# Last store moved from ScalarE to SyncE and two filler matmuls dropped in a SwiGLU feed-forward kernel

## The chip, the cores and the metric

One core of a Trainium2 chip. The metric is the device time of one execution in microseconds (us); lower is better. A time is the median of several executions, where not said otherwise. A profiled execution gives a span, from the first instruction to the last, which is about 1.3 us shorter than the time of the same execution. A run counts as slow when it is over 1.5% above the fastest of its kernel; the ratios are of fast runs alone, and the state of a single run is unknown.

A few words used below: the sequencer of an engine reads its instructions and starts them. A transfer is issued by an instruction on SyncE or ScalarE, and it has landed when its semaphore (the counter that others wait on) has its last increment. TensorE runs at half or at full clock: the 128-column fillers start 107 ns apart at half clock and 56 ns apart at full clock. The release is the moment at which the full clock is granted.

## The reference

```python
# x: 1 x 2048 x 640; w_gate, w_up: 640 x 1536; w_down: 1536 x 640; all bf16
def reference(x, w_gate, w_up, w_down):
    g = jax.nn.silu(x @ w_gate)
    u = x @ w_up
    return (g * u) @ w_down
```

## The kernel before

The 2048 rows of x are worked in four blocks of 512. In each block TensorE makes the gate tile `pg` and the up tile `pu` for 12 slices of 128 columns, ScalarE applies silu, VectorE multiplies, and TensorE then multiplies by w_down. The first block has no time to wait for a transposing load, so TensorE transposes x itself, and filler matmuls on a tile of ones (`warm`) fill the waits. The parts that matter here are the first and the last ones.

```python
    def warm(n):                      # fillers: their result is never read
        for _ in range(n):
            nc.tensor.matmul(pw[:, 0:P], lhsT=ones[:], rhs=ones[:], start=True, stop=True)
    ...
            if sb == 0 and fc == 0:   # the very first projection
                warm(N_WARM)          # 18
                transpose_chunk(0, [(dve, "po_a", 0, KD)])
                transpose_chunk(2, [(dve, "po_b", 0, KD)])
                warm(N_GAP)           # 2
                for c in (1, 3):
                    transpose_chunk(c, [(act, "po_a", 0, 2), (dve, "po_b", 2, KD)])
                warm(2)               # the two that the change drops
                proj_pair(pg, wg_sb, fc, sb, 0)   # ten matmuls of 256 columns in all
                proj_pair(pg, wg_sb, fc, sb, 1)
                proj(pu, wu_sb, fc, sb, 0, S_BLK)
    ...
        for j in range(SUB):          # output tiles of 128 rows
            ...
            nc.scalar.copy(ot[:], po_a[:])
            nc.sync.dma_start(out=out2[s0 : s0 + P, 0:DA], in_=ot[:])       # wide: 512 columns
            if last:
                # 12 matmuls of 128 columns into po_b
                nc.vector.tensor_copy(out=ot_b[:], in_=po_b[:])
                nc.scalar.dma_start(out=out2[s0 : s0 + P, DA:D], in_=ot_b[:])  # narrow: 128 columns
```

At the end SyncE alone waits for every semaphore (`_trim` moves all closing waits there) and clears them. The load queues are SyncE's and ScalarE's; the first tile of w_gate comes in two parts, three fifths on SyncE, two fifths on ScalarE.

## Time and profile before

| | before |
|---|---|
| time, first three runs | 164.18 us median (163.74 to 164.37) |
| span of the profiled run | 162.8 us |
| TensorE busy | 159.7 us, 98% of the span |
| first projection starts | 5.30 us |
| wide store's issue to the end of the span | 2.05 us |

The costliest groups of the page of before read as follows: line, engine, operation, tiles, shapes and count; then busy us and mean ns of one; then the idle time of the engine just before them and what ended it.

```profile
L198 PE MATMUL pu<-xT,wu_sb 128*128 128x512 bf16 (+1 forms) x240 | 59.5, 379 | 0.0
...
L245 ACT ACTIVATE sg<-pg 128x512 f32<-128x512 f32 (+1 forms) x48 | 28.6, 596 | 70.2 <-PE pg L198 65.7
```

TensorE's matmuls have no idle time before them (0.0). ScalarE sits idle for 70 us, nearly always until TensorE has filled a gate tile. So taking instructions from ScalarE gains nothing in the middle of this kernel; only its part in the very last stretch can count.

### The profile page before, as it was taken

Reading aid. Unit: us, or ns where it says so; the run is one execution under the profiler, and the core shown is the slowest. Engines: PE = TensorE matmul, PEld = TensorE weight load, DVE = VectorE, ACT = ScalarE, POOL = GpSimd, SP = SyncE. Lnnn points to the kernel's source line nnn. Section 1 sums busy time; section 2 is a strip of 40 time slices with the busy share of each in tenths; the row PEclk is TensorE's granted clock in tenths of the full one; section 3 lists DMA queues with packets and bytes.
Section 4 is the critical chain, followed back from the end, with each engine's and each line's share of the span. In section 5 each row is a group of like instructions: output and inputs, shape, how many; then the busy total and the mean of one; then the engine's idle time right before and its main releaser. Section 6 shows DMA issues by size and latency. Waiting matters only on the chain.

```text
span 162.8 us, 2081 instructions
## 1 busy us (share of the span) xinstructions
PE 159.7 (98%) x779; PEld 75.4 (46%) x779; DVE 111.8 (69%) x251; ACT 42.6 (26%) x73; POOL 0.6 (0%) x6
## 2 busy tenths in 40 slices
PE   8999999999999999999999999999999999999994
PEld 7644444444444444444444444444444444445442
DVE  2223333499559999979919999979964999993000
ACT  3322222212232222221222322221214222222121
POOL 1000000000000000000000000000000000000000
DMA  7999999993269993003110000000420000000312
GB/s 212 295 327 330 364 216 253 245 185 60 66 152 180 220 220 68 4 0 34 64 64 0 0 4 2 0 0 0 64 68 32 0 0 0 0 0 4 53 35 73
DMA packets 42585, 15.86 MB, mean 97 GB/s; under 512 B 33232, under 2 KB 42448, under 8 KB 42576
## 3 DMA queue, kind: packets, MB, share of 16 engines
q1 hardware_dynamic: 33664, 14.75, 37.2%
q10 hardware_dynamic: 8912, 0.98, 4.0%
q8 instruction: 6, 0.10, 0.3%
q14 instruction: 3, 0.02, 0.1%
HBM read 7.21 MB, written 2.62 MB: 60 GB/s over the span
## 4 chain that ended last, share of the span: by engine, by line
PE 95%; DMA 3%; SPq 0%; DVE 0%; issue 0%
PE pu L198 32%; PE pg L198 31%; PE po_a L281 25%; PE po_t L256 6%; DMA wg_sb<-in_w_gate_dram 3%; PE pg L213 1%; SPq L84 0%; PE po_b L298 0%; DVE ot_b L306 0%
## 5 line engine op out<-in xcount | busy, mean ns | idle before, releaser
L198 PE MATMUL pu<-xT,wu_sb 128*128 128x512 bf16 (+1 forms) x240 | 59.5, 379 | 0.0
L198 PE MATMUL pg<-xT,wg_sb 128*128 128x512 bf16 (+1 forms) x235 | 58.3, 379 | 0.0
L246 DVE TENSOR_TENSOR aT<-sg,pu 128x512 bf16<-128x512 f32 (+1 forms) x48 | 32.8, 683 | 32.0 <-PE pu L198 32.0
L245 ACT ACTIVATE sg<-pg 128x512 f32<-128x512 f32 (+1 forms) x48 | 28.6, 596 | 70.2 <-PE pg L198 65.7
L281 PE MATMUL po_a<-wd_sb,aT 128*128 128x512 bf16 x192 | 42.1, 379 | 0.0
L151 DVE SCALAR_TENSOR_TENSOR prod<-wgT,x_row 128x640 f32<-128x640 bf16 x48 | 39.4, 821 | 1.1
L151 DVE SCALAR_TENSOR_TENSOR prod<-wuT,x_row 128x640 f32<-128x640 bf16 x48 | 39.4, 821 | 1.0
L198 PEld LDWEIGHTS <-wu_sb 128*128 128x128 bf16 x240 | 23.5, 98 | 28.0
L198 PEld LDWEIGHTS <-wg_sb 128*128 128x128 bf16 x235 | 23.0, 98 | 27.6
L281 PEld LDWEIGHTS <-aT 128*128 128x128 bf16 x192 | 18.8, 98 | 22.5
L289 ACT CAST ot<-po_a 128x512 bf16<-128x512 f32 x16 | 9.4, 586 | 32.3 <-PE po_a L281 21.3
L256 PE MATMUL po_t<-aT,wd_sb 128*128 128x512 bf16 (+1 forms) x48 | 10.4, 366 | 0.0
L256 PEld LDWEIGHTS <-wd_sb 128*128 128x128 bf16 x48 | 4.7, 98 | 5.1
L306 DVE CAST ot_b<-po_b 128x128 bf16<-128x128 f32 x1 | 0.3, 291 | 9.9 <-PE po_b L298 9.9
L265 ACT CAST ot_t<-po_t 128x512 bf16<-128x512 f32 (+1 forms) x4 | 2.2, 560 | 11.6 <-PE po_t L256 11.6
L194 DVE COPY xT<-pt 128x640 bf16<-128x640 bf16 (+1 forms) x4 | 1.6, 425 | 3.4 <-PE pt L189 3.4
L151 DVE DVE_READ_ACCUMULATOR prod<-wuT,x_row 128x1 f32 x48 | 3.9, 82 | 0.0
L151 DVE DVE_READ_ACCUMULATOR prod<-wgT,x_row 128x1 f32 x48 | 3.9, 82 | 0.0
L267 DVE STREAM_TRANSPOSE ot_q<-ot_t 128x512 bf16<-128x512 bf16 (+1 forms) x4 | 2.7, 678 | 1.7 <-ACT ot_t L265 1.7
L180 PE MATMUL pw<-ones 128*128 128x128 bf16 x22 | 2.8, 304 | 0.4 <-DVE ones L104 0.4
L189 PE MATMUL pt<-ident,x_sb 128*128 128x128 bf16 x20 | 2.0, 268 | 0.5 <-DMA x_sb<-in_x_dram 0.5
L180 PEld LDWEIGHTS <-ones 128*128 128x128 bf16 x22 | 2.2, 143 | 0.4 <-DVE ones L104 0.4
(17 smaller groups left out, 9.0 us busy)
## 6 DMA issues: line engine op xcount, KB each, us to landing
out_dram<-ot SPq DMA_DIRECT2D x16, 128.0 KB, 1.7
wd_sb<-in_w_down_dram SPq DMA_DIRECT2D x1, 1920.0 KB, 12.6
wg_sb<-in_w_gate_dram SPq DMA_DIRECT2D x3, 480.0 KB, 7.1
wu_sb<-in_w_up_dram SPq DMA_DIRECT2D x3, 480.0 KB, 7.6
x_row<-in_x_dram SPq DMA_DIRECT2D x1, 640.0 KB, 4.8
out_dram<-ot_q ACTq DMA_DIRECT2D x12, 32.0 KB, 1.9
x_sb<-in_x_dram SPq DMA_DIRECT2D x2, 160.0 KB, 3.0
x_sb<-in_x_dram ACTq DMA_DIRECT2D x2, 160.0 KB, 3.2
```

The lines of the kernel that those rows point to most:

```text
L151: nc.vector.scalar_tensor_tensor(out=prod[:], in0=wT[:, fc, :], scalar=1.0, in1=x_row[:, t, :], op0=ALU.mult, op1=ALU.mult, accum_out=acc[ ...
L180: nc.tensor.matmul(pw[:, 0:P], lhsT=ones[:], rhs=ones[:], start=True, stop=True)
L189: nc.tensor.transpose(out=pt[:, kd - k0, :], in_=x_sb[:, c, kd * P : (kd + 1) * P], identity=ident[:],)
L198: nc.tensor.matmul(ps[:, c0:c1], lhsT=w_sb[:, kd, fc * P : (fc + 1) * P], rhs=xT[:, kd, sb * S_BLK + c0 : sb * S_BLK + c1], start=(kd == 0 ...
L213: nc.tensor.matmul(pair(ps[:]), lhsT=w_sb[:, kd, fc * P : (fc + 1) * P], rhs=pair(xT[:, kd, sb * S_BLK : (sb + 1) * S_BLK]), start=(kd == ...
L245: nc.scalar.activation(sg[:, 0:n_s], pg[:, 0:n_s], ACT.Silu)
L246: nc.vector.tensor_tensor(out=aT[:, fc, s_sl], in0=sg[:, 0:n_s], in1=pu[:, 0:n_s], op=ALU.mult)
L256: nc.tensor.matmul(po_t[:], lhsT=wd_sb[:, kf, DA:D], rhs=aT[:, kf, sb * S_BLK : sb * S_BLK + n_t], start=(kf == 0), stop=(kf == KF - 1),)
L265: nc.scalar.copy(ot_t[:], po_t[:])
L267: nc.vector.transpose(out=ot_q[:], in_=ot_t[:])
L281: nc.tensor.matmul(po_a[:], lhsT=aT[:, kf, s0 : s0 + P], rhs=wd_sb[:, kf, 0:DA], start=(kf == 0), stop=(kf == KF - 1),)
L289: nc.scalar.copy(ot[:], po_a[:])
```

## The change

The narrow last store goes to SyncE, so that ScalarE has no issue left to make after its last copy, and the two fillers ahead of the first projection go, so that it could start at once.

```diff
                 for c in (1, 3):
                     transpose_chunk(c, [(act, "po_a", 0, 2), (dve, "po_b", 2, KD)])
-                warm(2)
                 proj_pair(pg, wg_sb, fc, sb, 0)
...
-                nc.scalar.dma_start(out=out2[s0 : s0 + P, DA:D], in_=ot_b[:])
+                nc.sync.dma_start(out=out2[s0 : s0 + P, DA:D], in_=ot_b[:])
```

Nothing else moves: the compiled order of every engine is otherwise the same. Line numbers after the fillers are one lower in the changed kernel (L293 for L294).

## The prediction

> **What bounds the kernel now.** I read the front page first: the shares of the span by engine, then the chain that ended last.
>
> ```profile
> PE 159.7 (98%) x779; PEld 75.4 (46%) x779; DVE 111.8 (69%) x251; ACT 42.6 (26%) x73; POOL 0.6 (0%) x6
> ...
> PE 95%; DMA 3%; SPq 0%; DVE 0%; issue 0%
> ```
>
> TensorE is busy for 98% of a 162.8 us span, and 95% of the chain is TensorE work. The chain of work in order of time shows that it is one unbroken row of matmuls, each group of five taking 1.08 us. So only the two ends of the kernel can give or cost anything here: what precedes the first projection, and what follows the last matmul. Both parts of the change lie there. The start, first in the chain, then as a timeline from 4.7 us to 5.6 us (start, length, engine, line; in brackets the idle time before it and what ended it):
>
> ```profile
> 0.91 4.35 DMA wg_sb<-in_w_gate_dram
> 5.26 0.05 issue
> 5.30 0.72 PE pg L213 x5
> ```
>
> ```profile
> 4.72 0.66 DVE L194 COPY xT<-pt 128x384 bf16<-128x384 bf16 x2 [0.64 <-PE pt L189]
> 4.77 0.15 PEld L180 LDWEIGHTS <-ones 128*128 128x128 bf16 x2
> 4.83 0.28 PE L180 MATMUL pw<-ones 128*128 128x128 bf16 x2
> ...
> 5.30 0.33 PEld L213 LDWEIGHTS <-wg_sb 128*128 128x128 bf16 x4 [0.37 <-DMA wg_sb<-in_w_gate_dram]
> 5.30 0.50 PE L213 MATMUL pg<-xT,wg_sb 128*128 128x256 bf16 x3 [0.20 <-DMA wg_sb<-in_w_gate_dram]
> ```
>
> The reader is to see that the first projection does not wait for the fillers: they end at 5.11 us, then TensorE stands idle for 0.20 us (its weight loader for 0.37 us) until the first tile of w_gate has landed at 5.26 us. The end, as a timeline from 160 us on:
>
> ```profile
> 160.13 0.59 ACT L289 CAST ot<-po_a 128x512 bf16<-128x512 f32 x1 [2.05 <-PE po_a L281]
> 160.74 0.33 SPq L294 DMA_DIRECT2D out_dram<-ot  x1
> 160.76 0.29 DVE L306 CAST ot_b<-po_b 128x128 bf16<-128x128 f32 x1 [9.85 <-PE po_b L298]
> 161.08 0.36 ACTq L307 DMA_DIRECT2D out_dram<-ot_b  x1
> ```
>
> SyncE issues the last wide store (512 columns) from 160.74 to 161.07 us. VectorE has the last narrow tile (128 columns) ready at 161.05 us, and ScalarE, idle since 160.72 us, issues its store 0.03 us later. In the listing of DMA issues of that stretch (last column: us from issue to landing) the two stores are
>
> ```profile
> out_dram<-ot SPq DMA_DIRECT2D x1, 128.0 KB, 1.8
> out_dram<-ot_b ACTq DMA_DIRECT2D x1, 32.0 KB, 1.6
> ```
>
> so the wide one lands at 160.74 + 1.8 = 162.5 us and the narrow one at 161.08 + 1.6 = 162.7 us. The narrow store is the last thing to land; SyncE's closing instructions (L387) then add about 0.1 us to the end of the span at 162.8 us. Each microsecond by which that store starts later is a microsecond of the kernel, and nothing later covers it.
>
> **What the Trainium skill says.** Four places bear on this.
> "DMA: Bandwidth & Descriptors", section "Issuing engines are not separate DMA queues": initiating on several engines at once "will only save the time on the sequencer it takes to initiate the DMA, which is usually small relative to the DMA itself". The trace agrees: an issue is 0.33 to 0.36 us of a store that lands after 1.6 to 1.8 us. It is that sequencer time that the change gives up.
> "Perfetto Trace Analysis", section "DMA Instruction — HWDGE (DVE, Sync)": the block that generates descriptors is shared by the two issuing sequencers and locked for one at a time, and an issue's profiled time holds that lock wait but not the transfer. The trace allows it: the ScalarE store, issued just as SyncE's ended, took 0.36 us, SyncE's own 0.33 us. No run so far separates the two causes.
> "TensorE: Matmul & The Clock Gate", section "What's actually happening": the array runs at half clock until about 3.4 us of activity, judged in a free-running window, and falls back after an idle window of that length. The trace agrees on the first half: the first 18 fillers start 107 ns apart (2.10 us for 18 with the last one's 314 ns of latency), the last two 56 ns apart.
> The same page, section "Wait — 56ns, not 53.3ns?", predicts 55.8 ns between matmuls of 128 columns at full clock, which is what the trace has for these two.
>
> **The change part by part.** First, the two fillers. They are two matmuls of 128x128 with their two weight loads, 2 x 56 ns = 0.11 us of occupied array. They stand behind the last transposes and so delay none of the copies to xT; they write a scratch bank that nothing reads. Removed, TensorE reaches the wait on w_gate 0.11 us sooner and stands idle for 0.11 us longer, and the projection still starts at 5.30 us, because its weights land at 5.26 us. The load was issued at 0.91 us by a queue that does not wait for TensorE. Gain on the path: 0.00 us. It could become a gain only if w_gate landed more than 0.2 us earlier in other executions, and then at most 0.11 us.
>
> Second, the store. On SyncE it comes behind the wide store in program order. SyncE is free at 160.74 + 0.33 = 161.07 us. The compiled order of the changed kernel shows that the moved store waits for two semaphores (an earlier store's, and VectorE's for the tile); in the trace each store of the wide kind with two waits has a separate semaphore instruction of 17 ns ahead of it. The gap between two instructions of SyncE I take from the first loads in the chain: the first takes 0.39 us from 0.00, the next starts at 0.45 us, takes 0.41 us, and the third starts at 0.91 us, so 0.04 to 0.06 us. Two gaps and one 17 ns instruction are 0.10 to 0.14 us; one of the gaps may be less, so I take 0.10 us: the store starts at 161.17 us in place of 161.08 us, 0.09 us later. Its issue is about 0.03 us shorter if SyncE's 0.33 us holds for it, but it may be longer when the issue before it has just ended: the four ot_q stores of the last block, issued one right after another on ScalarE, took 0.32 us for the first and 0.48 us for the others, and landed after 1.6 us and 1.8 us. Those have 384 short pieces each, this store 128, so I expect 0 to 0.1 us of that, and take 0.03 us, which cancels the shorter issue. In the one queue the narrow store's packets come after the wide store's; the wide store's packets are nearly over when the narrow store's begin (0.8 to 0.9 us after issue in both), so the order costs nothing.
> Landing: 161.17 + 1.6 = 162.77 us, 0.09 us later. SyncE begins its closing waits 0.45 us later than before, at 161.55 us instead of 161.12 us, but four of them pass in under 0.3 us and the rest wait for landings at 162.5 us and later, so that is hidden. ScalarE saves 0.36 us of issue at a time when it has nothing else to do: 0.00 us.
>
> Sum: 0.00 - 0.00 + 0.09 = +0.09 us of span. On the time of 164.18 us that is 164.27 us, which I round to 164.3 us.
>
> **The rivals.** One: the serial issue costs more, 0.2 to 0.4 us, because the second issue in a row on one sequencer takes 0.48 us and its packets also queue behind 128 KB of the first. For it speak the ot_q stores; against it, that the first loads, of 128 pieces as here, took only 0.39 and 0.41 us in a row. It would make 164.4 to 164.6 us.
> Two: the narrow store gains, because on ScalarE it waited for the descriptor generator behind SyncE (0.36 against 0.33 us), or because the closing on SyncE follows it more directly. At most 0.05 us better than before, with the fillers perhaps 0.1 us: 164.1 us. Against it stands that VectorE's tile was ready at 161.05 us and the issue on ScalarE began 0.03 us later: there is hardly anything left to gain.
> Three: the fillers hold the clock up. Without them the idle time before the first projection grows from 0.20 us to 0.31 us; if the windows lie badly in some executions, the half clock lasts one window longer, and some of the first projections take twice as long: 3.4 us at half speed is 1.7 us, an estimate from the named page, 1% of the time. In the trace the full clock is there by 4.23 us, ahead of the fillers, and 0.31 us is far from an idle window. It would show in few executions, if in any: 166 us there.
>
> **Range and chances.** The repeats of the kernel before lie between 163.74 and 164.37 us, so their scatter of 0.6 us is wider than the effect. The range is the centre with that scatter and rival one on top: 163.8 to 164.8 us. For 2% the kernel would have to move by 3.3 us, which none of the rivals gives: chance of faster by over 2% is 0.01, within 2% 0.98, slower by over 2% 0.01.
>
> **What would show each step right or wrong.** Right for the fillers: the first projection still starts at about 5.3 us, its wait still names w_gate, now with about 0.3 us of idle TensorE, and its ten matmuls still start 109 ns apart (1.27 us for the ten). Right for the store: in the last microseconds two SyncE issues, the second starting at 161.15 to 161.2 us on the old clock, 0.4 to 0.45 us after the first, and landing about 1.6 us later; span about 162.9 us. Wrong would be: a first projection that starts earlier than 5.2 us, matmuls of twice the length after 5.3 us, a second issue of 0.45 us or more or landing after 1.8 us, or a gap after the last landing that differs from 0.1 us.

## The result

The changed kernel takes 164.10 us (median of six runs, 163.56 to 164.23); the kernel before, six runs, 164.05 us (163.74 to 164.37). The ratio is 1.000, with a 95% interval of 0.998 to 1.002. A ratio here is the mean time of one kernel's fast runs over the mean of the other's fast runs of the same rounds, so not quite the ratio of the medians. The time is the same.

The profiled run of the changed kernel happened to be the fastest of its six (163.56 us, span 162.2 us), half a microsecond under the median. Taken alone it looks like a gain. The busy shares and the chain of its page, then its chain from 4 us to 6 us in order of time:

```profile
PE 159.5 (98%) x777; PEld 74.8 (46%) x777; DVE 111.7 (69%) x251; ACT 42.7 (26%) x73; POOL 0.6 (0%) x6
...
PE 96%; DMA 2%; SPq 0%; DVE 0%; issue 0%
```

```profile
0.91 3.70 DMA wg_sb<-in_w_gate_dram
4.61 0.05 issue
4.65 1.26 PE pg L213 x10
```

Two matmuls and two weight loads are gone (777 for 779). The chain has the same shape: the first projection still follows the landing of w_gate by 0.05 us. But w_gate, whose issue starts at 0.91 us as before, took 3.70 us to land in place of 4.35 us. The end of the changed kernel, as a timeline, and the two stores in its listing of DMA issues:

```profile
159.56 0.59 ACT L288 CAST ot<-po_a 128x512 bf16<-128x512 f32 x1 [2.05 <-PE po_a L280]
160.17 0.33 SPq L293 DMA_DIRECT2D out_dram<-ot  x1
160.18 0.29 DVE L305 CAST ot_b<-po_b 128x128 bf16<-128x128 f32 x1 [9.85 <-PE po_b L297]
160.59 0.39 SPq L306 DMA_DIRECT2D out_dram<-ot_b  x1
```

```profile
out_dram<-ot SPq DMA_DIRECT2D x1, 128.0 KB, 1.7
out_dram<-ot_b SPq DMA_DIRECT2D x1, 32.0 KB, 1.5
```

The narrow store now starts 0.42 us after the wide one, not 0.34 us, its issue is 0.39 us long, not 0.36 us, and it lands 1.5 us after its start, not 1.6 us.

Cut at three instants (start of the first projection, of the first w_down matmul of block one, of the last wide store's issue), the two traces differ like this, in us:

| stretch | before | changed | difference |
|---|---|---|---|
| start to first projection | 5.305 | 4.653 | -0.652 |
| first projection to first w_down matmul | 25.923 | 25.996 | +0.073 |
| from there to the wide store's issue | 129.515 | 129.517 | +0.002 |
| wide store's issue to the end | 2.052 | 2.079 | +0.027 |
| span | 162.795 | 162.245 | -0.550 |

The gain lies wholly in the first row, 0.07 us of it is lost again by the first w_down matmul, and the store costs 0.03 us. Most of the 0.07 us is a second wait for w_gate: its next load landed at 6.84 us and the second gate tile started at 6.89 us, whereas in the trace of before that load (6.79 us) was long there when the tile began at 7.49 us. The experiments ask whether the first row belongs to the change.

### The profile page after: what moved, and what is told of

Its sections match the earlier page's. It is cut to its first block, busy times and chain, and to the rows that moved or that the text cites. A ratio compares the mean times of both kernels' runs of the same rounds, so it can differ in the third digit from the quotient of the medians.

```text
span 162.2 us, 2077 instructions
## 1 busy us (share of the span) xinstructions
PE 159.5 (98%) x777; PEld 74.8 (46%) x777; DVE 111.7 (69%) x251; ACT 42.7 (26%) x73; POOL 0.6 (0%) x6
## 4 chain that ended last, share of the span: by engine, by line
PE 96%; DMA 2%; SPq 0%; DVE 0%; issue 0%
PE pu L198 32%; PE pg L198 31%; PE po_a L280 26%; PE po_t L255 6%; DMA wg_sb<-in_w_gate_dram 2%; PE pg L213 1%; SPq L84 0%; PE po_b L297 0%; DVE ot_b L305 0%
```

## The experiments

### Each part alone, and both kernels again

These four ran on one chip. `e1_store_only` has the second half of the diff, `e2_fillers_only` the first; `e3_both_again` is the changed kernel, `e4_before_again` the kernel before, without any edit.

```diff
 # e1_store_only, against the kernel before
-                nc.scalar.dma_start(out=out2[s0 : s0 + P, DA:D], in_=ot_b[:])
+                nc.sync.dma_start(out=out2[s0 : s0 + P, DA:D], in_=ot_b[:])
 # e2_fillers_only, against the kernel before
-                warm(2)
```

> The store alone: the last narrow store goes to SyncE, the two fillers stay. My theory (a second issue on one sequencer starts later): the narrow store's issue starts 0.42 to 0.45 us after the wide store's, against 0.34 us on ScalarE, and it lands about 1.5 us later as in the changed kernel, so from the start of the wide store's issue to the end of the span it takes 2.07 to 2.10 us against 2.05 us before. Time within 0.1 us of the kernel before, ratio 1.000 to 1.001. Rival (the serial issue costs 0.2 us or more): that stretch is 2.25 us or longer.

> The fillers alone: the two fillers are dropped, the store stays on ScalarE. My theory (the first projection waits for w_gate, not for TensorE): the first projection starts within 0.1 us of the landing of w_gate's first tile, wherever that falls, the ten first matmuls stay 109 ns apart, and the end stretch is 2.05 us as before. Ratio 0.998 to 1.002. Rival (the fillers hold the clock up): first matmuls of twice the length in some run, a span about 1.7 us longer there. Rival (the fillers delayed the projection): 0.1 us faster in every run.

> The changed kernel once more, unchanged. The profiled run of the changed kernel was its fastest of six, 0.5 us under the median, and in it w_gate landed at 4.61 us in place of 5.26 us. My theory: that landing is chance, so this run has another value, between 4.5 and 5.6 us; the span minus the start of the first projection stays at 157.5 to 157.6 us. Rival (the change made the landing earlier): again 4.5 to 4.7 us here, and so in e2_fillers_only, but 5.2 us or later in e1_store_only and e4_before_again.

> The kernel before once more, for a second trace of it. If the landing of w_gate is chance, it may fall anywhere between 4.5 and 5.6 us here; the stretch from the start of the wide store's issue to the end of the span should be 2.05 us again, within 0.03 us, if the end does not depend on chance.

Times: the kernel before 163.87 us (11 runs; one of them, 166.28 us, is counted as slow and left out of the ratios), the store alone 163.98 us, ratio 1.0003 (0.9986 to 1.0021); the fillers alone 164.17 us, ratio 1.0010 (0.9990 to 1.0031); both again 163.87 us, ratio 0.9998 (0.9977 to 1.0019); the kernel before once more 164.25 us, one run. All the same. The traces say more. The end of the store alone and of the fillers alone, as timelines:

```profile
160.60 0.33 SPq L294 DMA_DIRECT2D out_dram<-ot  x1
160.62 0.29 DVE L306 CAST ot_b<-po_b 128x128 bf16<-128x128 f32 x1 [9.85 <-PE po_b L298]
161.03 0.39 SPq L307 DMA_DIRECT2D out_dram<-ot_b  x1
```

```profile
160.39 0.33 SPq L293 DMA_DIRECT2D out_dram<-ot  x1
160.41 0.29 DVE L305 CAST ot_b<-po_b 128x128 bf16<-128x128 f32 x1 [9.85 <-PE po_b L297]
160.73 0.36 ACTq L306 DMA_DIRECT2D out_dram<-ot_b  x1
```

With the store on SyncE the narrow issue comes 0.42 us after the wide one, on ScalarE 0.34 us, whatever the fillers do. The stretch from the wide issue to the end was 2.086 us for the store alone and 2.032 us for the fillers alone. That part follows the store and only the store, as expected.

In the trace of the fillers alone the projection started 0.05 us after w_gate had landed, its ten matmuls 109 ns apart, as expected.

The landing of w_gate's first part was at 5.12 us (store alone), 4.82 us (fillers alone), 4.61 us (both again) and 4.82 us (before again). The changed kernel thus had its first value again, where I expected another one and the rival (the change makes it land early) expected this. But that rival also wanted 4.5 to 4.7 us in the fillers alone, and 5.2 us or later in the two kernels with the fillers; the kernel before had 4.82 us here and 5.26 us in its first trace, and the later kernels that have these fillers, or more of them, had 4.20 to 4.86 us. So an early landing needs no change, and the 0.65 us of the first row is best read as chance.

One expectation was too simple. In the second trace of the kernel before the first projection was not held by w_gate: it could have started 0.02 us sooner by w_gate's landing. Its chain from 4 us to 7 us:

```profile
3.92 0.96 PE pt L189 x9
4.88 0.21 PE pw L180 x2
5.09 1.64 PE pg L213 x10
```

The chain is TensorE itself: transposes, then the two fillers, then the projection. The fillers take 0.21 us, not 0.11 us, and the ten first matmuls 1.64 us in place of 1.27 us. The array was still at half clock. This shows in the durations of the ten matmuls (min/median/max ns), first in the first trace of before, then in this one:

```profile
L213 PE MATMUL pg<-xT,wg_sb x10: 272/273/282, 5.3 to 6.3; 128*128 128x256 bf16 x10
```

```profile
L213 PE MATMUL pg<-xT,wg_sb x10: 272/381/421, 4.9 to 6.5; 128*128 128x256 bf16 x10
```

The matmuls start 213 ns apart until about 5.9 us and 109 ns apart after the trace's clock record grants full clock at 6.08 us. In the changed kernel's trace that record is at 3.12 us, in its second trace at 3.24 us. Between the two traces of before the kernel is the same; only the moment of release differs. The full clock then lasted 160.426 us in the changed kernel's trace and 157.013 us in this one. These are 47 and 46 times 3.4133 us: the clock changes at the borders of windows of that length, and their place differs between traces of kernels that start alike. The page "TensorE: Matmul & The Clock Gate" of the Trainium skill, section "What's actually happening", says just this (a free-running window of 3413 ns), and the records agree. So part of the scatter of all these kernels is the position of that window: this run of before lost 0.58 us in its first block (26.502 us from the first projection to the first w_down matmul, against 25.923 us in its first trace) although its projection started 0.42 us sooner.

### How many fillers are free, and what fillers do

```diff
 # e5_42_fillers, against the kernel before
-                warm(2)
+                warm(42)
 # e11_eight_fillers, against the kernel before
-                warm(2)
+                warm(8)
 # e6_no_fillers, against the changed kernel
-    N_WARM, N_GAP = 18, 2
+    N_WARM, N_GAP = 0, 0
```

> 42 fillers where the kernel before has two: 40 more of 56 ns are 2.22 us of array time. My theory (fillers fill a wait for w_gate of about 0.37 us of array time and only what goes beyond it costs): 2.22 - 0.37 = +1.85 us with the landing of the first trace, +1.2 to +2.0 us over the scatter of landings, ratio 1.008 to 1.012; the first projection starts right after the last filler and no longer waits for w_gate. Rival (fillers at this place are free, whatever their number, because the loads are the bound): within 0.3 us.

> Eight fillers in place of two: 6 more of 56 ns, 0.33 us of array time at full clock. Theory (they fill the wait for w_gate): the first projection still starts within 0.1 us of w_gate's landing if the wait was 0.33 us or more, at most 0.15 us later if not; ratio 0.998 to 1.002. If the clock is still at half when they run they take twice as long and cost up to 0.5 us in that run. Rival (each filler costs its array time): the projection starts 0.33 us after the landing, ratio 1.002.

> No fillers at all: the 18 at the start and the two between the transposes are gone too; the store on SyncE as in the changed kernel. My theory (the 18 at the start start the clock's window, the last two do nothing): the transposes and the first projections run at half clock, the full clock comes about 1.8 us later than in the trace of the changed kernel or at the next window, that is between 4.9 and 8.5 us[...]. Cost half of the half-clock time after the projection's start: +0.3 to +1.8 us. Rival (no filler matters because the loads are the bound): within 0.3 us, the projections at full clock from the start.

Of the kernel before, in the same rounds as 42 and none, the median was 163.82 us. 42 fillers: 166.22 us, ratio 1.0143 (1.0109 to 1.0177). The rival that fillers at this place are always free is out. The cost, 2.3 us, is also more than I expected (1.008 to 1.012), and for the profiled run (166.44 us) the chain from its start to 8 us says why:

```profile
5.01 2.79 PE pw L180 x42
7.80 0.22 PE pg L213 x2
```

w_gate had landed at 4.69 us and the full clock came at 5.82 us, so the first fillers ran at half clock, 107 ns each, and there was no wait left for them to hide in. Eight fillers: 164.33 us, ratio 1.0013 (0.9990 to 1.0035), inconclusive as a time. Its trace again fell on a late release: the eight fillers started from 4.64 to 5.37 us, mostly at half clock, with w_gate's two parts landed before them (4.20 and 4.63 us), so they delayed the projection by nearly 0.8 us. It started 1.2 us after w_gate's first part, not within the 0.15 us expected at full clock; a cost of up to 0.5 us was foreseen for this case.

No fillers at all: 164.66 us, ratio 1.0065 (1.0029 to 1.0102). The rival that no filler matters is out too. The ten first matmuls:

```profile
L213 PE MATMUL pg<-xT,wg_sb x10: 421/421/421, 4.6 to 6.6; 128*128 128x256 bf16 x10
```

All ten at half clock; the release came at 7.01 us, inside the range expected. The first projection started at 4.64 us, no later than in the changed kernel, so what is lost lies in the clock. That this trace did not just meet its windows badly, another trace shows: with both stores on ScalarE (below) a window ended at 3.61 us, here at 7.01 - 3.41 = 3.60 us; with the 20 early fillers the full clock came at that border, without them one window later. The 18 early fillers and the two between the transposes are worth 1.1 us by the times (0.65% of 164 us) in this design, by bringing the release forward; the last two are not. (Against the kernel before this run also has the store on SyncE, which is 0.04 us of it.)

### Sequencer or descriptor generator

A second issue on SyncE came later. Is that the sequencer, or would the descriptor generator, which the prediction names as shared by both queues, set the pace anyway? Cutting the narrow store into four makes the effect larger.

```diff
 # e7_four_sync, against the kernel before; e8_four_alternate: (scalar, sync, scalar, sync)
-                nc.scalar.dma_start(out=out2[s0 : s0 + P, DA:D], in_=ot_b[:])
+                for q, eng in enumerate((nc.sync, nc.sync, nc.sync, nc.sync)):
+                    eng.dma_start(out=out2[s0 + q * Q : s0 + (q + 1) * Q, DA:D],
+                                  in_=ot_b[q * Q : (q + 1) * Q, :])
```

> The last narrow store cut into four of 32 rows, all four on SyncE behind the wide one; fillers as before. My theory (each further issue on one sequencer comes about 0.43 us after the one ahead of it): the last one starts about 1.29 us after the first narrow one, the span grows by 1.1 to 1.4 us. If the issues of so small a store are shorter, 0.9 us. Rival (issues in a row are hidden by the landing time): under 0.3 us.

> The same four narrow stores, alternating ScalarE, SyncE, ScalarE, SyncE. If the serial resource is the sequencer (my theory): each has two, the last issue starts about 0.45 us after the first, the span grows by 0.4 to 0.6 us. If it is the shared descriptor generator (the rival): the issues stretch one another, to 0.6 us or more each, and the last one starts as late as with all four on SyncE, span +1.1 us or more.

Four on SyncE: 165.68 us, ratio 1.0111 (1.0084 to 1.0138). Alternating: 164.59 us, ratio 1.0051 (1.0023 to 1.0079). The ends of the two, as timelines, SyncE alone first:

```profile
160.97 0.33 SPq L294 DMA_DIRECT2D out_dram<-ot  x1
160.99 0.29 DVE L306 CAST ot_b<-po_b 128x128 bf16<-128x128 f32 x1 [9.85 <-PE po_b L298]
161.40 1.78 SPq L308 DMA_DIRECT2D out_dram<-ot_b  x4
```

```profile
160.53 0.33 SPq L294 DMA_DIRECT2D out_dram<-ot  x1
160.54 0.29 DVE L306 CAST ot_b<-po_b 128x128 bf16<-128x128 f32 x1 [9.85 <-PE po_b L298]
160.87 0.85 ACTq L308 DMA_DIRECT2D out_dram<-ot_b  x2
160.95 0.85 SPq L308 DMA_DIRECT2D out_dram<-ot_b  x2
```

Four issues in a row take 1.78 us; two and two beside one another take 0.85 us each. From the wide issue to the end it is 3.353 us with all on SyncE and 2.581 us alternating, against 2.04 us with one narrow store, so +1.31 us and +0.54 us. Both lie in the ranges of the sequencer theory and the second far from the rival's 1.1 us. By the times it is more, about +1.8 and +0.8 us; what exceeds the end stretch must lie ahead of it, and is not explained. Single issues lasted 390 to 419 ns in the row and 373 to 434 ns side by side, so two sequencers issuing at once hardly stretch one another. So most of an issue is serial on its sequencer alone. A short part in the shared generator is not excluded: the issues side by side started 0.08 and 0.10 us apart, and by an estimate from this only a part much longer than 0.1 us, at the same place in each issue, would have shown as a wait.

### Which queue the last two stores take

```diff
 # e9_swapped: wide on ScalarE, narrow on SyncE; e10_both_scalar: the first line only
-            nc.sync.dma_start(out=out2[s0 : s0 + P, 0:DA], in_=ot[:])
+            (nc.scalar if last else nc.sync).dma_start(out=out2[s0 : s0 + P, 0:DA], in_=ot[:])
-                nc.scalar.dma_start(out=out2[s0 : s0 + P, DA:D], in_=ot_b[:])
+                nc.sync.dma_start(out=out2[s0 : s0 + P, DA:D], in_=ot_b[:])
```

> For the size of the end stretch: the last wide store goes to ScalarE, the narrow one to SyncE, so each sequencer has one issue. On ScalarE the narrow store landed 1.58 us after its issue began, on SyncE behind the wide one 1.53 us. If each sequencer needs only be free, the narrow issue starts 0.34 us after the wide one, as in the kernel before, and the stretch from the wide issue to the end is 2.03 to 2.05 us if the shorter landing comes from lying behind the wide store, 1.99 us if it comes from SyncE's queue.

> Both last stores on ScalarE. If a second issue on one sequencer starts later whichever sequencer it is, the narrow issue starts 0.42 us after the wide one here too and the stretch from the wide issue to the end is 2.08 us, as with both on SyncE. If SyncE alone is slow at a second issue: 0.34 us and 2.04 us.

One look each, with the state unknown, so the times (164.01 and 163.77 us, before 164.18 us) tell nothing. The end of both on ScalarE:

```profile
160.35 0.36 ACTq L294 DMA_DIRECT2D out_dram<-ot  x1
160.36 0.29 DVE L306 CAST ot_b<-po_b 128x128 bf16<-128x128 f32 x1 [9.85 <-PE po_b L298]
160.81 0.39 ACTq L307 DMA_DIRECT2D out_dram<-ot_b  x1
```

The narrow issue comes 0.46 us after the wide one: a second issue waits on either sequencer, SyncE is not special. All arrangements, in us:

| wide, narrow on | traces | narrow issue after wide issue | narrow issue to landing | wide issue to end |
|---|---|---|---|---|
| SyncE, ScalarE (before) | 5 | 0.34 | 1.58 (1.577 to 1.587) | 2.040 (2.032 to 2.052) |
| SyncE, SyncE (changed) | 5 | 0.42 | 1.54 (1.527 to 1.550) | 2.084 (2.078 to 2.095) |
| ScalarE, SyncE (swapped) | 1 | 0.33 | 1.645 | 2.101 |
| ScalarE, ScalarE | 1 | 0.46 | 1.531 | 2.115 |

The five traces of the first row are the two of the kernel before and those of 2 (fillers alone), 42 and 8 fillers; of the second row the two of the changed kernel, the store alone, no fillers and the last experiment below. The landing is that of the last of the store's 16 semaphore increments. My expectation for the swap failed: neither 2.03 to 2.05 us nor 1.99 us, but 2.10 us. Still it answers its question: the landing is not shorter by SyncE's queue (1.645 us there with the queue to itself) but where the narrow store lies behind the wide one in one queue (1.53 to 1.54 us on either). Why is not shown, but the traces' packet records tell where the difference lies: in all twelve traces the store's last data packet ends 1.15 to 1.21 us after the issue starts, and the last increment follows 0.42 to 0.43 us later on a queue of its own, 0.36 to 0.38 us later behind the wide store. So it is not the wide store's packets that are in the way. ScalarE's wide issue took 0.36 us too, with none ahead of it, so 0.36 us is ScalarE's own length and not a wait for SyncE's issue. By these, with one trace each for the last two, the arrangement of before has the shortest end of the four.

### A start that does not wait for w_gate

If the landing of w_gate bounds the start, loading it ahead of half of x should help.

```diff
 # e12_weights_first, against the changed kernel
+    (first tile of w_gate, both parts)
     load_x(nc.sync, 1, 2)
     load_x(nc.scalar, 3, 4)
-    (first tile of w_gate, both parts)
     (first tile of w_up)
...
+                proj_pair(pg, wg_sb, fc, sb, 0)
                 for c in (1, 3):
                     transpose_chunk(c, ...)
-                proj_pair(pg, wg_sb, fc, sb, 0)
                 proj_pair(pg, wg_sb, fc, sb, 1)
```

> The changed kernel with the first tile of w_gate loaded ahead of the second and fourth chunk of x, and the first pair of projections (which needs only chunks 0 and 2 of x) ahead of the last transposes. If the landing of w_gate is the bound of the start, the first projection starts at 4.0 to 4.5 us in place of 4.6 to 5.3 us, but the last transposes now wait for x until about 4.5 to 5 us, so the second pair gains less; ratio 0.996 to 0.999. If the release of the clock or the later weights are the bound, the time is the same within 0.1%.

165.07 us against 164.18 us, ratio 1.0066 (1.0034 to 1.0099): slower, in every one of six runs (164.66 to 166.34 us), where I expected a gain or nothing. The profiled run is the second slowest of them (165.82 us). TensorE in its timeline from 3.3 us to 8.5 us:

```profile
3.35 0.42 PE L181 MATMUL pw<-ones 128*128 128x128 bf16 x2
4.57 1.25 PE L214 MATMUL pg<-xT,wg_sb 128*128 128x256 bf16 x5 [0.80 <-DMA wg_sb<-in_w_gate_dram]
5.61 1.27 PE L190 MATMUL pt<-ident,x_sb 128*128 128x128 bf16 x10
7.02 1.23 PE L214 MATMUL pg<-xT,wg_sb 128*128 128x256 bf16 x5
```

The first pair started at 4.57 us, hardly sooner, since w_gate still landed at 4.53 us, although its issue started at 0.45 us and not at 0.91 us; TensorE stood idle for 0.80 us before it; and the clock record grants full clock at 8.13 us only, so nearly everything in these lines runs at half speed. How much of the 0.9 us is the clock and how much the new order was not separated. No version that beats both kernels came out of this.

## Why the prediction was right or wrong

The time was predicted within 0.2 us and as the same, and it is. That alone proves little: the times scatter by 0.6 us, so a sum of 0.09 us can't be tested by them, and any small sum would have fitted. The traces test the steps. By its own steps:

**The store's later issue: right.** Predicted 0.09 us later; measured 0.42 - 0.34 = 0.08 to 0.09 us in five traces against five. The two gaps and the 17 ns semaphore instruction are there: in the changed kernel SyncE ends the wide issue at 160.50 us, runs the semaphore instruction at 160.54 us and starts the narrow issue at 160.59 us.

**The store's landing: mis-sized.** The step "take 0.03 us, which cancels the shorter issue" made the landing 1.6 us after the start as before. The issue itself became longer, not shorter (0.39 against 0.36 us), as it also does for the second on ScalarE (0.39 us), yet the landing came 0.045 us sooner after the start (1.54 against 1.58 us). The end grew by 2.084 - 2.040 = 0.044 us, half of the predicted 0.09 us. The rival with 0.2 to 0.4 us is out by the same row. The rival that the store gains is out as well, and so is its first reason, a wait for the generator, by ScalarE's 0.36 us with no issue ahead of it.

**Hidden closing waits and ScalarE's saved issue: right.** SyncE's closing waits start 0.48 us later relative to the wide issue (0.86 against 0.38 us), and the end does not move for it: in the traces of this comparison it comes 0.115 to 0.127 us after the last landing.

**The fillers cost nothing because w_gate lands later: right for the trace it was read from, wrong as a rule.** I took one execution's order of events for the kernel's. Of the seven traces with two fillers at that place (both of before, the store alone, the two with four stores, the two of the queues), three have the projection waiting for w_gate, but four have it right behind the fillers, 0.02, 0.08, 0.13 and 0.44 us after it could have started by w_gate. Of these delays the fillers' share is at most their own 0.11 us at full clock or 0.21 us at half clock. And the 0.08 us, of the swapped stores, came to nothing. Its chain from 0 to 8 us does not pass through the first projection:

```profile
2.66 4.62 DMA wg_sb<-in_w_gate_dram
7.28 0.05 issue
7.32 0.82 PE pg L198 x3
```

There the next load of w_gate landed at 7.28 us and held the second gate tile, whenever the first projection began. The mean over the seven is an estimate of what dropping the fillers gains: (0 + 0 + 0 + 0.02 + 0 + 0.13 + 0.21) / 7 = 0.05 us, and less, since array time freed at half clock is worth half of it at full clock (213 ns against 109 ns for one matmul). It would cancel part or all of the store's 0.044 us; neither is to be seen in times that scatter by 0.6 us, so the cancelling is argued, not shown. One of the prediction's signs of being wrong, a first projection earlier than 5.2 us, did come (4.65 us), but through the landing of w_gate and not through the fillers.

**The rival of the clock: its mechanism is real, its link to these two fillers was not found.** Fillers as a whole do bring the full clock forward (no fillers: +0.65%, release at 7.01 us), and the release moves from run to run between 3.1 and 6.1 us in the traces of these two kernels, which are the same up to the last transposes. But in the four traces without the two fillers and with the earlier ones unchanged the release came before the first projection in all but the reordered kernel. No run of the 18 timed without them (changed kernel twice, fillers alone) was slow. The kernel before had two slow runs, 166.28 and 166.65 us, among those of the experiments; no trace of such a run exists, so whether they are releases one window later stays open. Nor does their listed clock of 1.000 tell: the trace of the second run of before, released at 6.08 us, has 1.000 too.

**The range:** 163.8 to 164.8 us held the median. The scatter of the traced spans has its place at the start: from the first w_down matmul to the last wide store's issue it is 129.51 to 129.53 us in all fourteen traces. At the start it comes from the landings of w_gate (the first part at 4.2 to 5.3 us, issued at about 0.9 us in all traces but the last experiment's; the next load at 6.5 to 7.3 us) and from the position of the clock's window.

## What to carry to other kernels

Where the last two transfers of a kernel become ready within one issue time of each other, try them on two sequencers: a second issue on one started 0.08 us later here and moved the end by 0.04 us, and each further one, when several followed, came 0.45 us after the one ahead. For two transfers the gain is not assured: the swapped pair, on two sequencers too, had no shorter end than both on SyncE (2.10 against 2.08 us). Fillers ahead of a load wait are free only while the load is the later of the two, or while a later load holds the next step anyway, and whether it does can change from run to run with the landings and the clock, so look at several traces before calling an instruction hidden. And before explaining a faster profile, cut the span at fixed instants and check that the gain lies where the change is: here it all lay in a load that the change does not touch.

## What the Trainium skill lacked or had wrong

- "TensorE: Matmul & The Clock Gate", section "What's actually happening": it gives the window's length but not how busy the array must be in one for the release. Worked out here from the starts of the matmuls in the traces with a clock record (an estimate): windows with about 65% (kernel before, second trace), 63% (four on SyncE) and 70% (weights first) busy were not followed by the full clock, windows with about 78% and 83% (the two traces of the changed kernel) were.
- "Perfetto Trace Analysis", section "DMA Instruction — HWDGE (DVE, Sync)": it tells of one generator locked for exclusive use, with the lock wait inside the profiled issue, but not for how much of an issue it is locked. Two sequencers issuing at once showed no wait to speak of: 373 to 434 ns for each issue, beside 390 to 419 ns in a row on one. So the locked part is short beside the issue, or lies so that the two did not meet.
- "DMA: Bandwidth & Descriptors", section "Issuing engines are not separate DMA queues", gives no figure for the sequencer's time that it speaks of. The page has a cycle count for "previous generations" in its part on trn3, without naming trn2, and the skill elsewhere no more than an order of magnitude for the setup as a whole. The runs show it, from start to start, for a second issue right behind the first: 0.42 us on SyncE, 0.46 us on ScalarE, for stores of 128 rows, and 0.44 to 0.47 us for each further store of 32 rows.
